# A written-out order of all engines, searched again with later transfers

## The chip, the cores and the metric

The kernel runs on one core of one Trainium2 chip. The metric is the device time of one execution in microseconds (us), lower is better. A row of the profile counts its times from the first instruction of the span.

## The reference

Two stages follow each other, for 8 batches of 576 positions. Stage 1 is attention in a window of 64 positions, 8 heads of 64; its output, 576 x 512 per batch, is the input x of stage 2. Stage 2 is a mixture of four attention experts: a gate picks two of the four for each position, and each expert projects x to q, k and v of 64 columns, attends causally over all 576 positions and projects back to 512 columns. All inputs and the output are float32.

```
rel = pos[:, None] - pos[None, :]
scores = np.where((rel >= 0) & (rel < 64), q @ k.T / 8, -1e9)          # stage 1, per batch and head
x = softmax(scores) @ v                                                # 576 x 512 per batch
for e in range(4):                                                     # stage 2
    q, k, v = x @ wq[e], x @ wk[e], x @ wv[e]
    ye = softmax(causal(q @ k.T / 8)) @ v @ wo[e]
    out += gate_weight[e] * ye                                         # zero where e is not in the top two
```

## The kernel before

Stage 1 goes by groups of four blocks of 64 queries, 72 groups in all; stage 2 by batch and by pair of experts (pr 0 and 1). Products of stage 2 are made with float16 pairs (a high and a low part), so that each is three matmuls (`three`, lines 582 to 584).

All work is cut into *units*, each a Python generator whose steps issue instructions for one engine or two. No scheduler reorders anything: the table `ORDER` (lines 41 to 142) names the units one after the other, and each time that a name stands there, the next step of that unit is issued. After a colon stand the PSUM banks that the step takes. Each engine does its own instructions in the order of the table, and waits by semaphores for what they need from other engines and from transfers.

```
for x in ORDER.split():
    x, _, y = x.partition(":")
    ...
    banks[:] = map(int, y)
    next(units[x], None)
```

The names that matter here, with the lines of their instructions:

- `p15` loads q and k of two heads as they lie in pair 15 of 16 (lines 181, 183). `m67` makes the scores of a group or two on PE (line 339). `q67` is the softmax of a group (DVE, POOL, ACT), `t` turns its result on PE (line 405) and masks it on DVE (line 408), `a` multiplies with v (PE line 430), then ACT and DVE write x as a float16 pair (lines 455, 457).
- `h15` loads the v windows of pair 15 (lines 190, 191) into one of three tiles `vt`. `n7` finds the largest magnitude in the two v tiles of batch 7, a step for each tile: one DVE reduction over 1,280 columns (line 473). Batch b takes the tiles of `h` 2b and 2b+1. The first step of `n7` reads `h14`'s tile, the second `h15`'s.
- `M`, `N` make scales of that, `v`, `k` and `r` are the projections of stage 2 (first PE, 12 matmuls of 260, 320 or 256 columns, lines 582 to 584; then ACT lines 602, 665 and DVE lines 608, 673). `g` is the gate.
- `x` makes scores of stage 2 (PE line 707), `y` their masked minimum and exponential (DVE line 718, ACT line 722), `u` scales the weights and splits them into a high and a low half (ACT line 769, POOL lines 779, 780).
- `D4021` (batch 4, pair 0, part 2, half 1) turns such a piece from tile `sp` to tile `tu` by a DMA transpose that SP issues (line 790). Part 0 is read by `A400`, parts 1 and 2 by `A401`: the product with v on PE (line 829). Its first two thirds read the high halves (last digit 0), its last third the low ones. `o` is the output projection, with a store at its end (lines 858, 862).
- `Fa`, `Fb` are matmuls whose result nobody reads (line 871); `f`, `c`, `i` write constants.

SP issues all transfers but three, in the order of the table, and waits before each until its tile is free; one that waits holds up those behind it. A transfer also waits for the eighth before it, since eight semaphores are used in turn.

Of the kernel before, what the change touches and what calls it, by code (L numbers as in the profile page):

```python
# [41 lines left out]
    'p0 f:01234567 i c p1 h0 h1 l0 l2 Fa0_4:0 m0:7 p1 z m2:6 q0 p0 q2 l1 l3 Fa1_4:5 m1:5 q0 q0 h2 e1 q0 m3:3 q1 q0 q1 '  # L42
    'q3 q2 q1 q1 q2 q3 n0 q3 q3 n0 q3 q1 q1 w0 q1 q2 n0 q1 Fa2_17:0 M0:5 w0:7 M0 q2 q1 t1:3 w0 d w2 M0 t1 q3 w0 e0 '
    'Fb3_2:4 w2:4 w2 Fb4_2:0 a1:34 M0 w2 w0 m4:56 a1 m6:72 q3 q4 w2 w1 a1 m8:1 q3 q4 p2 q5 q3 w1:3 q6 w3 t3:4 q5 q4 '
    'p3 w2 w1 q4 Fb5_1:0 w3:3 t3 w1 w3 q5 q5 Fb6_5:0 a3:34 s n1 q4 q5 v00:0 N0 w3 q5 q8 q5 q6 q5 a3 q7 m9:65 w1 q6 w3 '
    'q6 q6 q7 q5 v00 t5:7 q8 a3 q8 q7 q8 w3 q9 v01:3 q7 t5 q7 q8 m11:42 q9 v00 q7 v01 q8 q7 m13:17 q10 q9 q7 q9 q12 '
    'p4 q8 q7 q9 t7:0 q10 q11 v01 q10 q8 q10 q11 q10 Fb7_1:6 t8:3 q12 t7 q12 q12 a5:56 q10 q10 q12 q11 q10 t8 m15:20 '
    'a5 q10 q11 a5 t10:3 k000:4 q11 t10 q12 q13 k000 q13 k000 q12 q16 q13 r000:3 q12 q13 q14 a7:45 q14 r000 q14 r000 '
    'q14 a8:67 a7 q14 h3 r010:3 k000 q13 a7 h4 a8 q12 a8 q14 r000 t12:4 q14 r010 q15 v02:7 q15 q16 t12 q16 b0 v02 '
    'r001:6 q16 q15 n1 q14 q15 v03:4 q14 q16 n2 r001 k010:0 v03 q15 v02 r010 q16 g00 x004:2 k010 m19:73 n1 g00 r001 '  # L50
    'v03 k010 y004 y004 M1:5 g00 x000:41 k010 M1 q20 m17:02 q16 r010 y000 y000 y000 M1 g00 q16 k001:6 y000 q16 q18 '
    't14:1 q17 r001 q19 k001 q17 k011:4 k001 g00 q18 p5 g00 M1 q18 q17 q18 N1 t16:5 q19 q20 q18 r011:6 q20 k001 q17 '
    'g00 q20 q17 g00 q19 q20 k011 q18 r011 x014:0 x002:23 y014 k011 q18 q19 g00 y002 x001:04 k011 q19 a10:23 g00 y001 '
    'r011 a10 r011 m21:67 t14 p6 q20 y001 x011:40 a10 q18 q18 q21 y014 Fb8_2:1 a14:23 u000 q22 u000 y011 t17:1 a14 '
    'u000 u000 m23:40 y011 u000 q20 t17 q20 q21 t19:1 a14 u000 q21 q21 u000 q23 a12:23 q22 q21 q23 q23 q22 u000 v10:6 '
    'h5 a12 t16 u000 q22 u000 a12 a16:45 t19 u000 q22 u000 D0000 x003:23 y003 m25:71 u000 u000 a16 y003 a16 x010:23 '
    'k100:5 u000 D0001 y010 u000 q26 y010 y010 v11:4 u000 n2 v10 y010 r100:3 v10 q20 q25 k100 u010 n2 v11 u010 q22 '
    'k100 D0010 v12:2 u010 v11 u010 r100 u010 u010 r100 M2:6 u010 u010 x104:3 v12 A000:4 y104 M2 q23 v12 u010 q24 M2 '
    'A000 m27:32 A000 u010 q22 a17:45 M2 u010 u010 q23 y104 h6 a17 a17 q22 D0100 r110:6 q22 t21:4 q24 q25 r110 q25 '
    'v13:5 b1 r110 q25 q27 t21 u010 q25 v04:6 u010 n3 u010 u010 D0101 k101:4 v04 D0011 v13 g04 k110:7 q24 q28 g04 q24 '  # L60
    'v04 u010 v13 q24 v04 g10 k101 x012:06 g04 r101:5 y012 D0111 g10 k101 g04 q24 r111:6 g10 r101 D0110 g10 g04 g10 '
    'r101 g04 k110 q24 g10 g04 g10 k110 x013:40 g10 q24 g10 r111 A010:5 y013 p7 N2 y013 x100:74 g04 r111 g10 g04 '
    't23:0 q26 y100 k111:6 A010 q26 q24 y100 y100 u001 g04 q26 x101:71 A010 y100 u001 u011 q26 o00:5 u001 q27 q26 '
    'u011 q26 u001 q27 y101 q26 o01:4 q27 q26 k111 u011 o00 u001 k111 t26:1 o01 x114:7 t26 m29:56 u001 y114 q27 t25:7 '
    'q28 q29 D0020 q28 q30 x110:14 u001 q28 q29 q30 u011 q29 y110 Fb9_2:3 x102:53 q28 y102 y110 q30 D0021 q28 x103:25 '
    'u011 y110 u011 q30 y103 D0120 x111:34 q30 a19:12 q28 u011 y111 y103 a21:56 t23 y101 A001:3 u101 D0121 t25 q28 '
    'a21 q28 m31:04 a19 u100 a21 p8 t28:7 y111 a19 a23:56 o00 u100 q31 o01 u100 A001 A011:1 q32 h7 u100 A001 u100 '
    'A001 q31 u100 u101 a23 q32 u101 a25:23 q29 u100 u101 a23 A011 q32 u101 x113:56 a25 u100 A011 o03:4 A011 q29 a25 '
    't28 o02:1 q30 u100 u100 y110 x112:73 u100 u100 D1000 o02 y112 o03 v20:2 u101 y113 u100 k200:3 v20 D1020 y113 n3 '
    'u101 r200:6 D1001 k200 n3 q30 v22:5 q30 D1021 r200 r200 q30 v20 t30:6 u100 u100 k200 v22 M3:1 m35:32 u100 v22 '  # L70
    't30 y114 m33:45 D1010 q32 u110 q31 u110 A100:7 M3 q31 u110 q32 u100 p9 q31 M3 v21:6 D1011 A100 u110 M3 A100 u110 '
    'u110 x204:7 a26:01 y204 u110 u110 q36 y204 k210:7 a26 h8 u110 u110 v21 a26 o03 v23:0 u110 u110 v21 k210 k210 '
    'x200:61 u111 v23 u110 u110 u111 y200 y200 k201:7 v23 u110 q33 D1101 r211:0 y200 u110 q34 y200 D1100 k211:6 n4 '
    'k201 u111 u110 u111 g20 r211 r201:1 k211 r211 g20 D1111 q35 u111 r210:0 u111 k201 r201 g20 r201 k211 D1120 q33 '
    'x201:17 r210 y201 A110:6 g20 q32 g20 o02 u111 y201 A101:1 D1110 r210 q34 q32 q34 A110 m37:70 A110 A101 D1121 q32 '
    'q34 A101 A101 x214:6 g20 q34 q38 o10:1 q33 y214 q32 q37 q33 g20 N3 q33 t32:6 q35 q36 q35 o11:5 q36 o10 q34 q35 '
    'q34 q36 q34 o10 q35 A111:1 q36 g20 q34 o11 q36 q36 y214 g20 o11 q36 t34:3 q37 A111 q38 q37 A111 m39:25 g20 q36 '
    'q37 q38 A111 q38 a30:01 q39 p10 q37 t35:7 q39 u200 a30 o12:4 q39 t35 b2 q39 q40 o13:7 q38 o12 u200 a30 u200 q38 '
    'u200 q39 o12 q38 u200 o13 a28:01 q38 u200 o14:2 t32 a28 q38 u200 u200 a28 t37:4 x211:76 o14 t34 u200 u200 a32:01 '
    'h9 y211 u200 u200 a34:23 a32 D2000 a32 x210:67 u200 u200 a34 t37 v30:0 y211 u200 D2001 a34 m41:41 u200 y210 y210 '  # L80
    'D2010 y210 a35:23 v32:6 q40 q42 u200 y210 n4 v30 q40 D2011 r300:7 u210 a35 q40 a35 b3 q40 u210 o14 q41 r310:2 '
    'v30 v32 u210 q40 q41 h10 q40 q41 u210 q40 r300 v32 o13 t39:0 q40 r310 v31:5 u210 u210 t39 v33:4 u210 u210 q42 '
    'v31 r310 q42 u210 n4 u210 r300 q42 v31 x202:20 u210 u210 x212:65 y202 q42 x203:73 y212 v24:2 v33 u210 u210 y203 '
    'q41 k301:5 u210 u210 n5 y203 D2110 M4:1 x213:70 k311:3 D2100 v24 u210 M4 k301 y213 k310:6 q41 g24 D2101 q42 q42 '
    'g24 g30 r301:0 q42 v24 k310 D2111 y213 k301 k311 g30 g24 v33 M4 q42 m43:57 M4 g24 v24 N4 g24 g30 r301 k300:2 q43 '
    'p11 g30 g24 g30 q43 g30 k311 u201 g24 q43 r301 r311:3 u211 q43 u201 g30 g24 g24 g30 k310 k300 g24 u211 q43 q44 '
    'g30 m45:06 r311 k300 u201 g30 u201 r311 x314:4 x304:1 q45 x301:25 u211 u201 u201 y301 A200:3 u211 D2020 A210:2 '
    'A200 y304 y301 A200 t41:1 q44 u211 y314 q44 x300:35 q45 A210 q44 A210 o20:4 u211 q44 y300 q45 q44 q45 o21:7 q46 '
    'u201 q44 q45 o20 y300 y300 x302:03 a37:45 y302 q44 o20 D2021 o21 m47:20 t41 u211 a37 x303:73 D2120 y300 a37 '
    't43:1 y303 a41:45 y304 q44 o21 y314 u300 q47 A201:3 q46 a41 u300 y303 D2121 u300 a41 q46 q48 t44:7 u300 v40:4 '  # L90
    'q47 q48 A201 t44 q48 q46 u300 A201 m49:75 q47 q46 A201 q48 a39:23 q49 q46 u300 q46 q46 A211:6 a39 t43 h11 u301 '
    'q48 u300 p12 u301 a39 a43:01 A211 u301 q46 u301 A211 o23:2 A211 a43 u301 u300 q50 a43 v40 o22:6 q47 u301 u300 '
    't46:0 q49 q50 n5 D3020 o22 v41:1 o23 q49 x310:26 t46 u301 q49 q49 q47 u300 x311:30 y310 v41 v42:7 u300 q50 u300 '
    'y311 y310 D3000 k410:3 q48 u300 u300 v41 y310 y311 D3021 k400:2 q48 u300 D3001 q50 y310 q50 v40 x312:16 q48 u300 '
    'm51:54 y312 q50 u310 v42 u300 a44:01 k410 k400 k410 q51 r400:6 h12 a44 q50 u310 q52 q48 D3011 a44 t48:3 q51 u310 '
    'k400 q50 u310 k401:0 o22 n5 u310 u310 v42 r400 q52 D3010 t48 q52 u310 u310 v43:7 q52 q52 n6 u310 u310 r410:3 v43 '
    'q51 k401 r400 u310 u310 q51 k401 g40 M5:2 m53:06 D3100 v43 r410 u310 u310 x404:7 k411:4 r410 y404 q51 M5 o23 q53 '
    'q54 q50 D3101 M5 x313:57 u310 u310 y404 M5 x400:13 k411 y313 D3110 y313 y400 r411:2 u310 k411 t50:7 q53 y400 q54 '
# [888 lines left out]
```

## Time and profile before

| | us |
|---|---|
| runs of the kernel before | 421.39, 419.54, 418.27; median 419.54 |
| the profiled execution | 419.1 |
| its span, from the first to the last instruction | 417.4 |
| PE busy with matmuls | 387.8 |
| DVE, ACT, POOL busy | 343.5, 331.8, 303.3 |

The profiled execution took 1.7 us beyond its span. "Busy" counts the time in which at least one instruction of the engine runs; matmuls are pipelined, so the end of one is modelled. The views below tell, for an engine's idle time, which instruction or transfer ended it. A row of the timeline reads: start, length, engine, line, operation, tile written and tiles read, shapes, count, and in brackets the idle time of the engine before it with what ended that.

### The profile page before, as it was taken

The numbers are of one execution on the slowest core, as the hardware profiler recorded it, in microseconds if no ns is written. First come the engines' busy times: TensorE is split into PE (matmuls) and PEld (weight loads), VectorE is DVE, ScalarE is ACT, GpSimd is POOL, SyncE is SP. The second block draws the span as 40 slices with busy tenths as digits, with TensorE's granted clock in tenths as the row PEclk, the third lists the DMA queues.
The fourth block names the chain that finished last, engine by engine and source line by source line (L and its number), as shares of the span: only waits on it lengthen the run. The fifth ranks groups of instructions, "written<-read, shape, count | busy, mean of one in ns | idle before, by whom it ended". The sixth has DMA issues, their size and how long they took to land. (4 is left out here: it accounts for less than half of the span.)

```text
span 417.4 us, 17928 instructions
## 1 busy us (share of the span) xinstructions
PE 387.8 (93%) x7108; PEld 291.4 (70%) x7108; DVE 343.5 (82%) x1044; ACT 331.8 (80%) x1150; POOL 303.3 (73%) x682
## 2 busy tenths in 40 slices
PE   8978999998899989999999997989899999999875
PEld 6856876785486866777677775678667876776554
DVE  5999899969997586898988898679787799689962
ACT  1978668975997868987899799677798689969962
POOL 7477557886978977888968987678787985977320
PEclk9999999999999999999999999999999999999999
DMA  7963333868499986789589977599918874599993
GB/s 250 361 220 127 121 109 124 146 120 185 93 196 214 277 185 205 128 175 226 104 174 214 198 119 204 193 207 187 203 73 161 142 125 88 129 164 172 176 186 126
DMA packets 141731, 71.02 MB, mean 170 GB/s; under 512 B 122576, under 2 KB 125648, under 8 KB 141648
## 3 DMA queue, kind: packets, MB, share of 16 engines
q1 hardware_dynamic: 141280, 69.50, 77.0%
q8 instruction: 55, 0.90, 0.9%
q10 hardware_dynamic: 368, 0.39, 0.3%
q14 instruction: 28, 0.23, 0.2%
HBM read 30.94 MB, written 9.44 MB: 97 GB/s over the span
## 5 line engine op out<-in xcount | busy, mean ns | idle before, releaser
L780 POOL TENSOR_TENSOR sp<-p,sp 128x320 f16<-128x320 f32 (+3 forms) x110 | 100.7, 916 | 9.2
L722 ACT ACTIVATE p<-p,r 128x448 f32<-128x448 f32 (+3 forms) x128 | 77.6, 613 | 5.2 <-DVE r L718 4.8
L769 ACT ACTIVATE sp<-p,r 128x192 f16<-128x192 f32 (+3 forms) x122 | 73.6, 623 | 4.9 <-POOL r L758 2.1
L367 ACT ACTIVATE p<-ps,st 128x64 f32<-128x64 f32 x204 | 61.5, 320 | 17.6 <-POOL st L364 17.3
L779 POOL TENSOR_SCALAR p<-p,r 128x320 f32<-128x320 f32 (+3 forms) x110 | 65.3, 594 | 9.8 <-ACT sp L769 8.4
L718 DVE CUSTOM_DVE_ANT_0 p<-ps,causal,sc 128x320 f32<-128x320 f32 (+2 forms) x128 | 63.5, 544 | 6.3 <-PE ps L707 4.9
L408 DVE TENSOR_TENSOR pt<-ps,tri 128x1024 f32<-128x1024 f32 (+1 forms) x40 | 44.2, 1107 | 5.7 <-PE ps L405 5.1
L392 POOL TENSOR_TENSOR p<-p,st 128x256 f32<-128x256 f32 x72 | 43.6, 614 | 6.7 <-DVE st L388 5.1
L829 PE MATMUL ps<-tu,v 128*64 128x64 f16 (+2 forms) x1056 | 39.3, 229 | 4.6 <-DMA tu<-sp 3.8
L367 ACT ACTIVATION_READ_ACCUMULATOR p<-ps,st 128x1 f32 x204 | 43.5, 213 | 0.0
L707 PE MATMUL ps<-kt,qt 64*128 64x320 f16 (+3 forms) x480 | 40.6, 292 | 2.5 <-DVE v L608 1.2
L829 PEld LDWEIGHTS <-v 128*64 128x64 f16 x1056 | 35.8, 111 | 9.8 <-issue 5.7
L339 PE MATMUL ps<-k,q 64*32 64x96 f32 (+2 forms) x2304 | 37.5, 245 | 4.7 <-DMA k<-in_kT_dram 1.7
L582 PE MATMUL ps<-xh,wqhi 128*128 128x256 f16 (+1 forms) x128 | 36.6, 286 | 3.2 <-DVE qt L673 2.3
L430 PEld LDWEIGHTS ps<-pt,vt 64*64 64x64 f32 x1440 | 33.7, 133 | 7.5 <-issue 1.8
L430 PE MATMUL ps<-pt,vt 64*64 64x128 f32 (+1 forms) x1440 | 38.1, 249 | 0.7 <-DVE largest L271 0.4
L339 PEld LDWEIGHTS ps<-k,q 64*32 64x32 f32 x2304 | 29.9, 106 | 11.3 <-issue 5.2
L582 PE MATMUL ps<-xh,wkhi 128*128 128x320 f16 (+1 forms) x128 | 36.6, 286 | 0.0
L584 PE MATMUL ps<-xh,wklo 128*128 128x320 f16 (+1 forms) x128 | 36.6, 286 | 0.0
L583 PE MATMUL ps<-xl,wkhi 128*128 128x320 f16 (+1 forms) x128 | 36.6, 286 | 0.0
L584 PE MATMUL ps<-xh,wqlo 128*128 128x256 f16 (+1 forms) x128 | 36.6, 286 | 0.0
L583 PE MATMUL ps<-xl,wqhi 128*128 128x256 f16 (+1 forms) x128 | 36.6, 286 | 0.0
(167 smaller groups left out, 1027.2 us busy)
## 6 DMA issues: line engine op xcount, KB each, us to landing
vt<-in_vW_dram SPq DMA_DIRECT2D x16, 576.0 KB, 5.9
q<-in_qT_dram SPq DMA_DIRECT2D x14, 576.0 KB, 4.9
k<-in_kT_dram SPq DMA_DIRECT2D x14, 576.0 KB, 6.0
out_dram<-out SPq DMA_DIRECT2D x30, 256.0 KB, 3.5
tu<-sp SPq DMA_TRANSPOSE x93, 4.5
out_dram<-out SPq DMA_DIRECT2D x9, 128.0 KB, 2.6
q<-in_qT_dram SPq DMA_DIRECT2D x2, 320.0 KB, 7.0
k<-in_kT_dram SPq DMA_DIRECT2D x2, 320.0 KB, 6.5
```

The lines of the kernel that those rows point to most:

```text
L339: nc.tensor.matmul(S1[g][o:o + 32, i, c:c + n], lhsT=q_t[r, i % 2, q0:q0 + 32], rhs=k_t[r, i % 2, k0:k0 + n], start=True, stop=True)
L367: nc.scalar.activation(pt[:, i], ps[:, i, 64:128], AF.Exp, bias=st[:, 0, z + i:z + i + 1], scale=0.125, accum_out=st[:, 1, z + i:z + i + 1])
L430: nc.tensor.matmul(to, lhsT=values[d][r, h, b + e - (w == 0)], rhs=rhs, start=(e, h) not in started, stop=s == n - 1, skip_group_check=True)
L582: nc.tensor.matmul(ps, lhsT=ah, rhs=bh, start=first, stop=False)
L583: nc.tensor.matmul(ps, lhsT=ah, rhs=bl, start=False, stop=False)
L584: nc.tensor.matmul(ps, lhsT=al, rhs=bh, start=False, stop=last)
L718: nc.vector.tensor_tensor_reduce(out=dst, in0=src, in1=mask, scale=SC[b][:, 3:4], scalar=above, op0=OP.add, op1=OP.min, accum_out=to)
L722: nc.scalar.activation(p, p, AF.Exp, bias=r2[:, 0, x:x + 1], scale=-1.0, accum_out=r2[:, 1, x:x + 1])
L769: nc.scalar.activation(hi, p, AF.Copy, scale=by)
L779: nc.gpsimd.tensor_scalar(p, p, by, 1.0, op0=OP.mult, op1=OP.mult)
L780: nc.gpsimd.tensor_tensor(lo, p, hi, op=OP.subtract)
L829: nc.tensor.matmul(to, lhsT=V2[b % 2][:, c, a, 2 * pr + h], rhs=rhs, start=n == 0, stop=n == len(work_list) - 1, skip_group_check=True)
```

## The change

Only the table `ORDER` differs: the sequence of the steps on all engines and the PSUM bank numbers. Every unit, tile and instruction is the same, but for the matmuls that nobody reads: 40 calls before, 32 now. The change says of itself that the new sequence was searched with every transfer counted as landing later than on the mean.

The table is replaced as a whole. Here stand the lines that hold `h15` and the second `n7` (the load of a v tile and the reduction that reads it), of the table before and of the new one:

```diff
-    'a61 u510 q64 o43 h15 u510 u500 a61 m67:70 a59 D5000 q65 u510 x503:56 a59 q65 v62:1 u510 u510 y503 D5010 u510 '
-    'u510 y503 q66 v61:5 q67 D5001 q64 u510 n7 v62 r600:6 v61 u510 u501 q68 q66 q65 q64 q66 k600:3 u501 v62 u501 r600 '
...
+    'u500 a61:34 q65 a59 q65 m67:10 a59 u500 a61 q66 x503:56 u500 a61 D5001 k600:7 q65 u510 h15 y503 u500 y503 q65 '
+    'o42 u510 q66 D5010 x513:34 y513 r610:6 k600 u510 q64 u510 q66 k600 o43 y513 u510 q64 q68 q64 q67 v61:7 q64 u510 '
+    't64:4 q67 q68 r610 u510 v62:3 v61 u501 t64 v61 u510 q66 u510 u510 v60:5 v62 u510 r610 u510 n7 v60 r600:6 D5100 '
```

A name with a colon issues matmuls; between `h15` and this `n7` the table before has four of them (m67, x503, v62, v61), the new one six (x513, r610, v61, t64, v62, v60).

DVE around that reduction (tile `mv_7` from tile `vt0`), in the table before:

```order
L351 COPY_PREDICATED ps_67<-win_91,ps_67 128x2x64
L351 COPY_PREDICATED ps_67<-win_91 128x2x64
L473 TENSOR_REDUCE mv_7_5649<-vt0_84 128x1
L354 COPY_PREDICATED ps_67<-win_91,ps_67 128x4x64
L378 TENSOR_REDUCE st1_65_6378<-p1_65_6379 128x4
L756 RECIPROCAL r2_1_120<-r2_1_120 128x2
L608 SCALAR_TENSOR_TENSOR v2_0_116<-ps_67,v2_0_116 128x256 x2
L673 SCALAR_TENSOR_TENSOR qt0_105<-ps_67,qt0_105 128x320
L362 TENSOR_REDUCE st1_67_6551<-ps_67 128x4
```

DVE around the same reduction in the new table:

```order
L372 TENSOR_REDUCE st1_67_6519<-ps_67 128x4
L408 TENSOR_TENSOR pt1_64_6542<-ps_67,tri_92 128x1024
L608 SCALAR_TENSOR_TENSOR v2_0_116<-ps_67,v2_0_116 128x256
L673 SCALAR_TENSOR_TENSOR qt1_106<-ps_67,qt1_106 128x320
L473 TENSOR_REDUCE mv_7_5587<-vt0_84 128x1
L374 TENSOR_TENSOR p1_68_6522<-ps_67,st1_67_6519 128x256
L608 SCALAR_TENSOR_TENSOR v2_0_116<-ps_67,v2_0_116 128x256
L756 RECIPROCAL r2_1_120<-r2_1_120 128x2
```

One of the two evictions of v (line 608) and one of a projection of q (line 673) now stand ahead of the reduction; before, all of them stood behind it.

SP around the load of q and k of pair 13 (`q13`, `k13`), which stage 1 reads in `m57`, in the table before:

```order
L790 DMA_TRANSPOSE tu10_82<-sp10_77 128x11x128
L790 DMA_TRANSPOSE tu11_83<-sp12_79 128x8x128 x2
L790 DMA_TRANSPOSE tu11_83<-sp11_78 128x10x128 x2
L181 DMA q13_5158<-in_qT_dram 128x2x576
L183 DMA k13_5159<-in_kT_dram 128x2x576
L862 DMA out_0_dram<-out_3_0_5166 128x512
```

SP around the same load in the new table:

```order
L790 DMA_TRANSPOSE tu10_82<-sp10_77 128x11x128 x2
L790 DMA_TRANSPOSE tu11_83<-sp12_79 128x8x128
L181 DMA q13_4865<-in_qT_dram 128x2x576
L183 DMA k13_4866<-in_kT_dram 128x2x576
L790 DMA_TRANSPOSE tu11_83<-sp12_79 128x8x128
L790 DMA_TRANSPOSE tu11_83<-sp11_78 128x10x128 x2
```

The load has moved ahead of three transposes (one of tile `sp12`, both of `sp11`).

## Rows read from the trace of the kernel before

**Rows 1.** The page, part 1: busy time of each engine.
```profile
PE 387.8 (93%) x7108; PEld 291.4 (70%) x7108; DVE 343.5 (82%) x1044; ACT 331.8 (80%) x1150; POOL 303.3 (73%) x682
```
**Rows 2.** The waits: engine, line, waited for, us, times, longest.
```profile
DVE mv L473 <- DMA vt<-in_vW_dram: 9.7, 8, 2.0
...
PE ps L829 <- DMA tu<-sp: 3.8, 3, 1.5
```
**Rows 3.** The timeline of DVE: reductions of v that waited for their load.
```profile
52.63 1.49 DVE L473 TENSOR_REDUCE mv<-vt 128x1 f32<-128x1280 f32 x1 [1.12 <-DMA vt<-in_vW_dram]
...
93.10 1.49 DVE L473 TENSOR_REDUCE mv<-vt 128x1 f32<-128x1280 f32 x1 [1.69 <-DMA vt<-in_vW_dram]
...
147.12 1.49 DVE L473 TENSOR_REDUCE mv<-vt 128x1 f32<-128x1280 f32 x1 [1.78 <-DMA vt<-in_vW_dram]
...
233.74 1.49 DVE L473 TENSOR_REDUCE mv<-vt 128x1 f32<-128x1280 f32 x1 [0.57 <-DMA vt<-in_vW_dram]
...
272.86 1.49 DVE L473 TENSOR_REDUCE mv<-vt 128x1 f32<-128x1280 f32 x1 [1.11 <-DMA vt<-in_vW_dram]
...
319.76 1.49 DVE L473 TENSOR_REDUCE mv<-vt 128x1 f32<-128x1280 f32 x1 [1.98 <-DMA vt<-in_vW_dram]
```
**Rows 4.** The timeline of PE: idle times that a DVE instruction ended.
```profile
54.50 1.00 PE L339 MATMUL ps<-k,q 64*32 64x96 f32 x64 [0.56 <-DVE v L608]
...
96.24 0.56 PE L707 MATMUL ps<-kt,qt 64*128 64x320 f16 x5 [1.20 <-DVE v L608]
...
149.26 0.30 PE L582 MATMUL ps<-xh,wqhi 128*128 128x320 f16 x1 [1.32 <-DVE qt L673]
...
236.01 1.00 PE L339 MATMUL ps<-k,q 64*32 64x96 f32 x64 [0.48 <-DVE kt L673]
...
275.54 0.27 PE L582 MATMUL ps<-wvhi,xt 128*128 128x260 f16 x1 [1.13 <-DVE pt L408]
...
323.08 0.30 PE L582 MATMUL ps<-xh,wqhi 128*128 128x320 f16 x1 [1.02 <-DVE qt L673]
```
**Rows 5.** The timeline of PE: idle times that a transfer ended, and one beside.
```profile
30.18 0.96 PE L339 MATMUL ps<-k,q 64*32 64x32 f32 x64 [0.96 <-DMA k<-in_kT_dram]
...
258.25 0.43 PE L339 MATMUL ps<-k,q 64*32 64x32 f32 x24 [0.71 <-DMA k<-in_kT_dram]
260.46 0.39 PE L582 MATMUL ps<-wohi,y 128*128 128x512 f16 x1 [1.78 <-DVE pt L408]
...
299.85 0.41 PE L829 MATMUL ps<-tu,v 128*64 128x256 f16 x4 [1.49 <-DMA tu<-sp]
...
399.45 0.63 PE L829 MATMUL ps<-tu,v 128*64 128x256 f16 x12 [1.07 <-DMA tu<-sp]
...
404.46 0.45 PE L829 MATMUL ps<-tu,v 128*64 128x256 f16 x10 [1.20 <-DMA tu<-sp]
```
**Rows 6.** The page, part 6: transfers, count, KB each, median us from issue to landing.
```profile
vt<-in_vW_dram SPq DMA_DIRECT2D x16, 576.0 KB, 5.9
...
k<-in_kT_dram SPq DMA_DIRECT2D x14, 576.0 KB, 6.0
...
tu<-sp SPq DMA_TRANSPOSE x93, 4.5
```
**Rows 7.** The timeline of PE: two v projections, then one of q, then k.
```profile
315.53 0.28 PE L582 MATMUL ps<-wvhi,xh 128*128 128x260 f16 x1
...
318.20 0.30 PE L582 MATMUL ps<-xh,wqhi 128*128 128x320 f16 x1
...
319.83 0.30 PE L582 MATMUL ps<-xh,wkhi 128*128 128x320 f16 x1
```
**Rows 8.** The timeline of PE at the start: matmuls that nobody reads.
```profile
4.51 1.92 PE L871 MATMUL ps<-px 128*128 128x128 f32 x8
...
10.38 4.06 PE L871 MATMUL ps<-px 128*128 128x128 f32 x34
```
**Rows 9.** The page, part 2: granted clock in 40 slices.
```profile
PEclk9999999999999999999999999999999999999999
```

195 rows, old and new, of the table ORDER are left out of this document.

## Prediction

> **What bounds the kernel now.** I read the busy times first: PE is busy for 387.8 of the 417.4 us of the span, DVE for 343.5, ACT and POOL for less [rows 1]. So PE is the bound, and 29.6 us of its span is idle. Matmuls and their number stay, but for some that nobody reads, so a new order can only win idle time of PE: at the very most 29.6 us, and less, since at both ends of the span PE has no work yet or no more.
>
> Next I read who waits for transfers, since the change counts these as later. The list of waits has two such groups of weight. DVE waits 9.7 us in 8 places, at the reduction `n` (line 473), for the load of the v tile; PE waits 3.8 us in 3 places for a transposed piece `tu` [rows 2]. The reader is to see that the larger group is not PE's: it costs nothing until PE runs out of work.
>
> Then the timeline, to see whether PE does. Six reductions wait, at 52.63, 93.10, 147.12, 233.74, 272.86 and 319.76, for 0.57 to 1.98 us, 8.25 us together [rows 3]. Two to four us behind each, PE stands and is released by a DVE instruction that the order puts behind that reduction: 0.56, 1.20, 1.32, 0.48, 1.13 and 1.02 us, 5.71 us together [rows 4]. PE stands some 70% as long as DVE did; the rest was hidden by work that PE still had. Last come PE's own waits for transfers: 0.96 and 0.71 us for k, and 1.49, 1.07 and 1.20 us for `tu`, 5.43 us together [rows 5]. So 11.1 us of the 29.6 us goes back to transfers. The wait of 1.78 us at 260.46 [rows 5], two us behind the late k, is put down to DVE; I do not count it to the 11.1.
>
> **The loads of v.** Both orders have 16 loads and 16 reductions; what changes is how much PE work the order puts between them. I count that work by the spacing of such steps in the trace: from one step of v to the second after it 2.67 us, so 1.3 us for a v step, and 1.6 us for a q step [rows 7]; other steps likewise. For `h15` and the second step of `n7`, the table before has m67 0.6, x503 0.4, two v steps 2.6: 3.6 us. The new table has x513 0.4, r610 1.6, two steps of `t` 0.4 together with two v steps and one more 3.9, thus 6.5 us by unrounded spacings. A load takes 5.9 us from issue to landing in the median [rows 6]; 3.6 is too little, and the reduction waited 1.98 us. (3.6 + 1.98 = 5.6, so the two views agree.)
>
> By the same count, the six reductions of [rows 3] go, in order of time: from 4.4 to 6.8 us, from 4.7 to 4.7, from 6.0 to 12.2, from 3.1 to 6.5, from 4.0 to 8.7 and from 3.6 to 6.5. Five of them pass 5.9 us; the second, `h6` to the first half of batch 3, does not move. I therefore take away five of the six idle times of [rows 4], 0.56 + 1.32 + 0.48 + 1.13 + 1.02 = 4.5 us, and leave the 1.20 at 96.24. Two of the five pass by only 0.6 us, and a load that is issued late because SP is held up is not seen in such a count. The bounds for this term are 2 us (only the two large leads, and half the rest) and 5.7 us (all six).
>
> The Trainium skill has a rule against this term. Its page "DMA: Bandwidth & Descriptors", section "Anatomy of one DMA — SWDGE (gpsimd) path", gives one transfer about 2.0 us of fixed cost plus its bytes at 436 GB/s, for 576 KB an estimate of 2.0 + 1.35 = 3.4 us. By it nearly every lead of before would have been long enough, the waits would have other causes, and the new order would gain nothing here. The trace disagrees: such loads took 5.9 and 6.0 us [rows 6], and these six readers did wait; the measurement decides.
>
> **PE's own waits for transfers.** k at 30.18: the lead falls from 5.0 to 4.4 us, so its 0.96 us stays and may grow by 0.6. k at 258.25 is pair 13, which SP now issues three transposes earlier, and its readers stand later: the lead goes from 4.9 to 16.2 us, and 0.7 us goes. `tu` at 299.85 is `D4021`, whose lead goes from 2.8 to 4.1 us, and the low half is read last; of the 1.49 us I take 1.2 away. A transpose lands 4.5 us after its issue in the median [rows 6], so 4.1 is near enough to leave something. The two at the tail: for 399.45 the pieces of batch 7, pair 0 lose as much lead as they win (one from 3.5 to 3.0, one from 5.0 to 3.0, one from 3.5 to 6.0), for 404.46 one goes from 1.6 to 2.5, the other from 4.0 to 2.5. I take nothing for these 2.3 us, with bounds of 1 us won and 2 us lost. Over all 96 pieces the mean lead is the same (11.6 and 11.7 us), but 9 instead of 18 lie under 4 us, so no new wait of this kind is likely.
>
> **What the new order puts in their place.** Every step moved brings its other waits along. Counted in the two orders, PE has 212 places where it can wait for DVE before and 207 now; in 94 before and 107 now it has no work of its own between the step that gives DVE its input and the one that takes the result. The trace does not have the new places, so the price of one lies between nothing and what PE loses here when DVE is late, 0.5 to 1.3 us [rows 4]. Even with DVE held for 8.25 us [rows 3], 30% stayed hidden, and DVE is idle for 18% of the span [rows 1], so most of the 13 more should cost nothing. I take two of them, at the lowest of the six prices: 2 × 0.5 = +1.0 us, a choice rather than a reading. Bounds: −1 us (the 5 places fewer may take waits of their own away) and +3 us (the two at the highest price).
>
> **Dummy matmuls, start and end.** Forty calls that nobody reads become 32. They are only worth something if they are not hidden; all but the first lie in front of work for which PE would otherwise wait, so taking them out turns busy time to idle time, and the sum takes 0. At the start 8 calls (before: 8 in two groups, then 17) [rows 8] stand ahead of the first scores; POOL writes one constant before the tile that they read. With them at 0.24 us each as at first, or twice that, and the constant ahead or beside, I work out for the first scores between 1.1 us earlier and 1.4 us later: 0, with these as bounds. At the end both orders have the same chain of output, 0.
>
> **The sum.** Of the profiled execution's 419.1 us: − 4.5 (v loads) − 0.7 (k) − 1.2 (`tu`) + 1.0 (new places) + 0 (start, tail) = **413.7 us**. The profiled execution lies 0.4 us below the median of the three runs, 419.5, so nothing is to be put right. About 1% (4.2 us) can be told from no change here; 413.7 is 1.4% below, just outside.
>
> **The rivals.** *More goes.* The 1.78 us at 260.46, the 1.20 at 96.24 and the tail go too: all of 11.1 + 1.8 us, with the places at nothing: 406 us, and up to 410. For it speaks that a search looked at all transfers; against it, that three leads stay under the landing time.
>
> *No change.* The waits were not what set the time: DVE's reduction comes on time, and PE then waits for the next thing in the same stretch, DVE's own queue. For it: DVE is busy 82% of the span, and PE's gaps are shorter than the waits before them, so a part is already slack. If the DVE term gives 2 us instead of 4.5, with the bounds +1.5 more elsewhere, it is 419.1 − 2 − 1.9 + 2.5 = 417.7. The skill's rule above ends here too, at 419.
>
> *Slower: PE on the heels of DVE.* The order is laid for late transfers, and PE steps now follow closer on DVE steps. If all 13 more places cost 0.85 us, the middle of 0.48 to 1.32 [rows 4], it is 419.1 − 6.4 + 11 = 423.7 us. It decides where more than seven such places show a wait (7 × 0.85 = 6). Against it: the largest of PE's gaps behind DVE, those of [rows 4] and the 1.78 of [rows 5], all stand shortly behind a late transfer.
>
> *Slower: a cold start.* PE's granted clock shows 9 in all slices [rows 9], with the many dummy matmuls at the start; the first eight took 0.24 us each, the later ones 0.12 [rows 8], so PE began at half pace, 1.2 of 2.4 GHz, and was at full pace by 10.4. With 17 calls fewer ahead of the first scores it could go longer at half pace. If the first 30 us did so, some 12 us of matmuls would cost twice as long, and some 6 us of that would fall into idle time: about 425 us.
>
> **How the numbers follow.** Forecast, 0.52, own range 410.5 to 416.5: most of it (0.40) is faster by over 1% (below 415.3), the rest (0.12) within. More goes: 0.09, faster. No change: 0.24, within 1%. DVE's heels: 0.11, of which 0.10 is slower by over 1% (above 423.7) and 0.01 within. Cold start: 0.04, slower. Thus faster 0.49, same 0.37, slower 0.14. For the range I go from 408.5, which leaves out the better part of the first rival, to 421.5, which leaves out the two slower ones and holds no change.
>
> **What would show it.** Right: DVE's waits for v loads fall from 9.7 us to 3 or less, one is left near 95 us, and PE's idle times behind them are gone; the scores of pair 13 do not wait for k; PE's waits for `tu` lie at the tail only; PE's idle time is about 24 us. Wrong: DVE's waits go but PE's idle time stays near 30 us, with other releasers (no change); PE's waits for DVE (lines 408, 608, 673, 718) grow, and no DVE wait for a transfer stands ahead of them (heels); matmuls of the same shape before 35 us last twice as long (cold start). A load that is issued later than its place, because SP stands before a transpose, would show as a wait of the reduction in spite of a long lead.

## The result and the profile after

The changed kernel takes 415.82 us in the median of 14 runs (412.69 to 417.47), the kernel before 420.47 us in as many: a ratio of 0.9884, 95% interval 0.9849 to 0.9918. That is 1.2% faster, 4.65 us between the medians, where 5.4 us were forecast. The profiled execution took 415.31 us, with a span of 413.6 us, 3.8 us less than before.

Page, part 1, and a row of its part 3, of the changed kernel:

```profile
PE 386.8 (94%) x7092; PEld 288.8 (70%) x7092; DVE 340.3 (82%) x1044; ACT 332.6 (80%) x1150; POOL 301.8 (73%) x682
...
q8 instruction: 55, 0.90, 0.9%
```

PE is busy 1.0 us less than in [rows 1] and idle for 413.6 − 386.8 = 26.8 us instead of 29.6. The sum went down by only 2.8 us, but what it consists of has changed. Part of it is hidden by the matmuls that nobody reads: they alone kept PE busy for 10.1 us before and 7.2 us after (counted from the traces). Without them, the time in which PE does no useful work fell by 5.7 us, from 39.7 to 34.0, and the useful matmuls took 1.9 us longer, 379.6 instead of 377.7; together that is the 3.8 us of the span. The waits of the changed kernel (engine, line, waited for: us, times, longest):

```profile
PE ps L339 <- issue: 5.9, 3, 2.6
PE ps L214 <- DVE half L207: 3.0, 1, 3.0
PE ps L829 <- DMA tu<-sp: 2.1, 4, 1.4
PE ps L405 <- ACT p L367: 1.9, 2, 1.1
PE ps L405 <- POOL p L392: 1.9, 4, 0.6
DVE mv L473 <- DMA vt<-in_vW_dram: 1.3, 2, 1.0
PE ps L797 <- ACT sp L769: 1.1, 2, 0.9
```

The waits of DVE for v fell from 9.7 us [rows 2] to 1.3. Summed by the engine waited for, PE's waits for DVE fell from 14.3 to 6.3 us (3.0 of these, and 1.1 of those before, are the very first instruction, which has nothing ahead of it to hold up), those for transfers from 5.5 to 2.1. Against that stand waits for ACT, from 1.1 to 4.1 us, for POOL, from 1.1 to 1.9, and the first row: idle time that the profile ends with nothing, from 1.6 to 5.9 us. The wait for `tu` at A401 is still there, as in [rows 5]:

```profile
295.91 0.52 PE L829 MATMUL ps<-tu,v 128*64 128x256 f16 x6 [1.44 <-DMA tu<-sp]
```

The largest wait of PE without a cause stands in the middle of one step, m55, after 39 of its recorded matmuls. Timeline of PE in the changed kernel (start, length, instruction, count, idle time before):

```profile
240.80 1.29 PE L829 MATMUL ps<-tu,v 128*64 128x256 f16 x32
242.01 0.27 PE L480 MATMUL ps<-ident,mv 128*1 128x128 f32 x1
242.21 0.58 PE L707 MATMUL ps<-kt,qt 64*128 64x320 f16 x6
242.73 0.75 PE L339 MATMUL ps<-k,q 64*32 64x96 f32 x39
246.10 0.54 PE L339 MATMUL ps<-k,q 64*32 64x96 f32 x25 [2.63 <-issue]
246.57 0.44 PE L582 MATMUL ps<-wohi,y 128*128 128x512 f16 x1
246.80 0.63 PE L583 MATMUL ps<-wolo,y 128*128 128x512 f16 x1
247.23 0.63 PE L584 MATMUL ps<-wohi,y 128*128 128x512 f16 x1
```

Behind it the matmuls of 512 columns follow each other at 0.43 us, and the busy time by stretch (PE, PEld, DVE, ACT, POOL, granted clock, share of DMA, GB/s) says why:

```profile
240.00:246.80 6.80, 4.17 (x138) 3.21 (x135) 4.64 (x18) 5.57 (x24) 5.67 (x10) 1.00 1.22 173
246.80:250.20 3.40, 3.40 (x12) 1.39 (x12) 1.71 (x7) 0.79 (x2) 0.24 (x1) 0.50 0.49 110
```

For 3.4 us the granted clock is 0.50, the lower level of 1.2 GHz. A second such stretch begins at 397.0, behind waits of 0.94 and 0.46 us at line 797, where PE itself turns the last pieces by matmuls. Until its last matmul, the profile before has no such stretch; so some of the 1.9 us that the useful matmuls took longer lies here.

### The profile page after: what moved, and what is told of

Read it like the earlier page. It is cut to its first block, busy times and chain, and to the rows that moved or that the text cites. A ratio compares the mean times of both kernels' runs of the same rounds, so it can differ in the third digit from the quotient of the medians.

```text
span 413.6 us, 17936 instructions
## 1 busy us (share of the span) xinstructions
PE 386.8 (94%) x7092; PEld 288.8 (70%) x7092; DVE 340.3 (82%) x1044; ACT 332.6 (80%) x1150; POOL 301.8 (73%) x682
## 5 line engine op out<-in xcount | busy, mean ns | idle before, releaser
L722 ACT ACTIVATE p<-p,r 128x192 f32<-128x192 f32 (+3 forms) x128 | 77.4, 609 | 9.9 <-DVE r L718 9.6
L769 ACT ACTIVATE sp<-p,r 128x448 f16<-128x448 f32 (+3 forms) x122 | 73.4, 620 | 3.8 <-POOL r L758 2.6
L392 POOL TENSOR_TENSOR p<-p,st 128x256 f32<-128x256 f32 x72 | 43.6, 617 | 13.4 <-DVE st L388 10.8
L829 PE MATMUL ps<-tu,v 128*64 128x64 f16 (+2 forms) x1056 | 39.7, 231 | 2.1 <-DMA tu<-sp 2.1
L582 PE MATMUL ps<-xh,wkhi 128*128 128x256 f16 (+1 forms) x128 | 36.7, 287 | 0.0
L584 PE MATMUL ps<-xh,wklo 128*128 128x256 f16 (+1 forms) x128 | 36.6, 286 | 0.0
L583 PE MATMUL ps<-xl,wkhi 128*128 128x256 f16 (+1 forms) x128 | 36.6, 286 | 0.0
```

Of the source, the lines that this page charges most:

```text
L582: nc.tensor.matmul(ps, lhsT=ah, rhs=bh, start=first, stop=False)
L583: nc.tensor.matmul(ps, lhsT=ah, rhs=bl, start=False, stop=False)
L584: nc.tensor.matmul(ps, lhsT=al, rhs=bh, start=False, stop=last)
L722: nc.scalar.activation(p, p, AF.Exp, bias=r2[:, 0, x:x + 1], scale=-1.0, accum_out=r2[:, 1, x:x + 1])
L769: nc.scalar.activation(hi, p, AF.Copy, scale=by)
L829: nc.tensor.matmul(to, lhsT=V2[b % 2][:, c, a, 2 * pr + h], rhs=rhs, start=n == 0, stop=n == len(work_list) - 1, skip_group_check=True)
```

## The experiments

The theory to be tested was that of the forecast: late loads of v hold DVE, PE stands behind it, and the new order wins by giving these loads time. Its rivals were that PE would have waited for DVE in any case, or that the gain lies elsewhere. In the pieces of the table below, "-" is the old place and "+" the new one. Each run gives a ratio to the kernel before on the same chip.

**after_again, after_3: the changed kernel twice more.** No edit.

> The changed kernel once more, as the measure for the runs beside it. Both theories: about 416 us, 1.2% under the kernel before. If PE's stall of 2.63 us in the middle of m55 (at 246.10 in the first profile) comes from where the program's text lies, it stands there again, at about 2.6 us, and so does the one of 1.55 us in m23 at 69.92; if these were accidents of one execution, they are gone or elsewhere.

> The changed kernel a third time, as the measure for the runs beside it: about 415 us. All theories: the stalls in m55 (1.9 to 2.6 us so far) and m23 (1.3 to 1.6 us) stand there again, and 3.4 us at half clock behind the one in m55.

Measured: 0.9895 (0.984 to 0.995) and 0.9864 (0.9818 to 0.9909). The stall in m55 was 1.87 and 1.93 us, always with 25 recorded matmuls behind it, each time with half clock right after; the one in m23 1.26 and 1.23 us. So these belong to the program, not to one execution. A401 waited again for D4021, 1.41 and 1.43 us, and in after_again also 1.56 us for D4020 just ahead of it. One wait for v had stayed in the changed kernel and grew: that of the reduction which stood at 233.74 before [rows 3]. It was 1.03 us in the first profile, 1.70 and 1.86 in these two, and here PE stood behind it again, for 0.87 and 1.04 us. Timelines of DVE and PE in after_3:

```profile
226.47 1.49 DVE L473 TENSOR_REDUCE mv<-vt 128x1 f32<-128x1280 f32 x1 [1.86 <-DMA vt<-in_vW_dram]
```

```profile
228.41 0.30 PE L582 MATMUL ps<-xh,wqhi 128*128 128x320 f16 x1 [1.04 <-DVE qt L673]
```

**b_late_n: the reductions later.** One of the six places (the others alike):

```diff
- q67 D5001 q64 u510 n7 v62 r600:6 v61
...
- u501 u510 r610:6 t64 k600
...
+ u501 u510 r610:6 n7 t64 k600
```

> The table before with one thing changed: the six reductions of v that waited for their loads come later, so that 8 to 10 us of PE work lie between load and reduction (before 3 to 6). Theory (the waits of these reductions make PE's six idle times): DVE's waits for v fall from 9.7 to under 3 us, the six idle times of 5.7 us go, and the time falls by 4.5 to 5.7 us, 1.1 to 1.4%. Rival (PE would have waited for DVE in the same places anyway): the waits go, the time stays within 1.5 us of before, and PE's idle time stays near 30 us with other releasers.

Measured: 1.0022 (0.9986 to 1.0058), no gain at all, although DVE's waits for v fell to 1.1 us. The rival had it right for this run. The timeline of DVE in this kernel shows where the reduction of 96 us went, and the timeline of PE what came of it:

```profile
96.06 1.47 DVE L473 TENSOR_REDUCE mv<-vt 128x1 f32<-128x1280 f32 x1
...
98.31 0.55 DVE L718 CUSTOM_DVE_ANT_0 p<-ps,causal,sc 128x320 f32<-128x320 f32 x1
```

```profile
98.92 0.27 PE L582 MATMUL ps<-xh,wqhi 128*128 128x256 f16 x1 [1.85 <-DVE m L718]
```

The 1.20 us at 96.24 [rows 4] are gone, but 1.5 us of reduction now stand ahead of the two operations of line 718 for which PE waits next, and that wait grew from 0.62 to 1.85 us. This is one place of six; the others were not followed up. Behind the first 45 us, in which the two tables are the same, PE was idle for 17.1 us until its last matmul instead of 18.8. The run took away the wait and moved 1.5 us of DVE's work at once; it doesn't tell the two apart. The next one does.

**b_no_wait: the same order, other data.**

```diff
-values[2 * b + x]
+values[2 * b + x - ((b, x) in ((2, 0), (3, 0), (4, 0), (6, 0), (6, 1), (7, 1)))]
```

> The table before, with the six reductions of v that waited for their loads reading the tile of the pair before, which lies there long since; the order of all engines is untouched. (Left out by this: six scales come from other data.) Theory (the waits make PE's idle times behind them): DVE's waits for v fall to some 1.5 us, PE's six idle times of 5.7 us go, 1.1 to 1.4% less time. Rival (what the late n run showed: PE waits for the next thing instead, since DVE has its own work to catch up): the waits go, but PE's idle time falls by under 2 us, and the time by under 0.5%.

Measured: 0.9929 (0.9888 to 0.997), 3.0 us less (1.3 to 4.7). Page, part 1, and the waits:

```profile
PE 386.6 (94%) x7107; PEld 291.1 (71%) x7108; DVE 344.0 (84%) x1044; ACT 331.8 (81%) x1150; POOL 303.0 (74%) x682
```

```profile
PE ps L829 <- DMA tu<-sp: 3.1, 3, 1.5
...
PE ps L582 <- DVE pt L408: 1.8, 1, 1.8
DVE mv L473 <- DMA vt<-in_vW_dram: 1.4, 2, 1.0
```

The span was 410.3 us, so PE was idle for 23.7 us: 5.9 less than before, and all six idle times of [rows 4], 5.7 us, are gone from its timeline. The waits of DVE do make PE's. In time it came to about two thirds of the 4.5 us that were forecast for five of the six, with an interval that holds them, and to half of the 5.7 us of idle time, which the interval leaves out. The profile is of one of the shortest executions, 413.12 us, at a granted clock of 0.999. The 1.8 us of line 408 that are left are those at o33.

**a_early_n and a_late_h: the waits put back into the new table.** First with the reductions forward (one of five places), then with the loads back:

```diff
-r610 u510 n7 v60 r600:6 D5100
...
-q67 v61:7 q64 u510 t64:4
...
+q67 v61:7 n7 q64 u510 t64:4
```

> The new table with five of these reductions moved forward until the lead over their loads is that of the table before (3.4 to 6.3 us of PE work). Theory: the waits come back to some 7 us in five places, PE stands behind them for 4 to 5 us, and the time rises by 4 to 5 us over the new table, to about the time before. Rival (the gain of the new table has another source): within 1.5 us of the new table.

```diff
-D5001 k600:7 q65 u510 h15 y503 u500
...
-q67 v61:7 q64 u510 t64:4
...
+q67 v61:7 h15 q64 u510 t64:4
```

> The new table with five loads of v moved back (h4, h8, h12, h13, h15) until the lead is 2.7 to 5.9 us of PE work; the order of PE, DVE, ACT and POOL is untouched. Theory: waits of some 7 us come back, PE loses 4 to 5 us, so 1.0 to 1.2% over the new table. Second theory (from the run with early reductions, which lost 17 us): in the new order DVE and PE stand so close that a late reduction costs PE more than its wait, and the clock with it: 7 to 15 us, 1.7 to 3.5%. Rival (loads don't matter): within 1.5 us of the new table.

Measured: a_early_n 1.0314 (1.0259 to 1.0369), 17.8 us over the new table run beside it, which neither theory had. a_late_h 0.9932 (0.989 to 0.9973), about 0.5% over the new table's 0.9884, in the direction of the theory, but with half of its size, and the intervals overlap: that later loads alone cost time in the new order is not shown. The waits of the two, a_early_n first:

```profile
DVE mv L473 <- DMA vt<-in_vW_dram: 10.8, 4, 3.3
PE ps L582 <- DVE xl L457: 7.2, 2, 3.9
...
PE ps L707 <- DVE kt L673: 3.1, 3, 2.7
PE ps L582 <- DVE qt L673: 2.3, 1, 2.3
```

```profile
DVE mv L473 <- DMA vt<-in_vW_dram: 7.2, 3, 3.4
...
PE ps L582 <- DVE p L374: 2.6, 1, 2.6
PE ps L430 <- DVE v L608: 1.7, 1, 1.7
```

In a_early_n the reductions stand in another place of DVE's work as well. Its 10.8 us of waits and the moved work cost PE 13.3 us in five gaps, one of them (1.06 us) behind a reduction that did not wait. Five stretches of 3.4 us at half clock lie in the span ahead of the last matmuls, three of them at these gaps and one behind the stall in m55, and the clock granted over it is 0.977. How much of the 17.8 us is wait, place and clock was not taken apart. The profile of a_late_h is of its longest execution, 420.61 us, at a granted clock of 0.981; it shows the waits, and not the time of the median run. In a_late_h, where DVE's order is that of the new table, three of five loads came late. One of the three waits, 1.55 us, is no longer than the changed kernel has there without this edit (1.03 to 1.86 us); behind the other two PE lost 4.3 us. Two loads with a lead of 4.3 and 5.9 us came in time, one with 4.6 us, behind the load of pair 14 and a transpose on SP, made a wait of 3.4 us: PE work between load and reader alone doesn't tell the landing.

**b_p13 and b_p13_3: q and k of pair 13 earlier.** Past seven transposes, and past three:

```diff
- o31:5 q56 g40 A301 p13 q52 q53 y414 A301 o30 t52:1
...
+ M5:2 m53:06 p13 D3100 v43 r410
```

> The table before with the load of q and k of pair 13 moved ahead, behind m53, past seven transposes on SP. Theory: PE's wait of 0.71 us at m57 goes, and the 1.78 us at o33 two us behind it stays, 0.2% less. Rival: the 1.78 us was a consequence of the late k (m57, then its softmax and t52 on DVE stood back): both go, 2.5 us or 0.6% less. A third way: the transposes behind it on SP come later, and A301 or A311 waits for them by as much.

```diff
- o31:5 q56 g40 A301 p13 q52 q53 y414 A301 o30 t52:1
...
+ q54 r401:4 y400 p13 D3111 r411
```

> The table before with the load of pair 13 moved ahead of three transposes only, as in the new table, behind the piece that A310 waits for. Theory (the 1.78 us at o33 followed from the late k, and the loss of b_p13 was the 3.3 us wait of A310 for its transposed piece): the waits at m57 and o33 go, none comes at A310, and the time falls by 2 to 2.5 us, 0.5 to 0.6%. Rival: another transposed piece comes late by as much, and the time stays within 0.2% of before.

Measured: b_p13 1.0053 (1.0017 to 1.0089), b_p13_3 0.9863 (0.9803 to 0.9923). Both waits went together in both runs, that for k and the 1.78 us at o33. In b_p13 another took their place (timeline of PE), and the timeline of SP has its cause:

```profile
249.89 0.78 PE L829 MATMUL ps<-tu,v 128*64 128x256 f16 x17 [3.31 <-DMA tu<-sp]
```

```profile
239.90 1.65 SPq L790 DMA_TRANSPOSE tu<-sp  x1
241.60 1.08 SPq L862 DMA_DIRECT2D out_dram<-out  x1
242.78 9.56 SPq L790 DMA_TRANSPOSE tu<-sp  x5
```

The piece that A310 waits for was issued at 242.78 and landed at 249.85, 7.1 us later, where the median is 4.5 [rows 6]. In the kernel before it stood first in this row of the timeline of SP and landed at 242.09:

```profile
237.60 13.45 SPq L790 DMA_TRANSPOSE tu<-sp  x5
```

So it landed 7.8 us later: 5.2 us because SP issued it later (1.0 us of that is how late SP already was 15 us earlier, ahead of the moved load), and 2.6 us because it took longer. The third way that the expectation named is what happened, at A310 instead of A301 or A311. Three transposes later (b_p13_3) there is no such wait; m57 runs through:

```profile
256.31 0.94 PE L339 MATMUL ps<-k,q 64*32 64x96 f32 x64
```

The time fell by some 1.4%, more than the 0.6% expected. The trace accounts for 2.1 us of it (PE's idle time is 413.3 − 385.8 = 27.5 us instead of 29.6), and for 2.0 us less of busy time; with six runs the interval reaches from 0.8 to 2.0%, and what lies beyond 2.5 us stays unexplained. This one moved load thus measures what the whole new table measures beside it, 0.9864, and the two can't be told apart. Sums of idle time are coarse, too: in the first 45 us, which all runs of the old order share, PE was idle for 6.6 us in the profile before and for up to 8.4 in the others.

**b_all: all three at once.** b_no_wait and b_p13, and A401 behind the first step of o40:

```diff
- y510 u411 A401:0 q63 A410 A400 A410 A400 y510 o40:6 M6
...
+ y510 u411 q63 A410 A400 A410 A400 y510 o40:6 A401:0 M6
```

> All three removed together in the table before: the six waits of the reductions (other data, as above), k of pair 13 loaded ahead, and A401 behind the first step of o40. Theory (my sum without its price for new places): 6.4 us less, 1.5%, thus as fast as the new table or faster. Rival: what the new order gained lies in how PE and DVE follow each other and not in the transfers; then under 2.5 us, 0.6%.

Measured: 0.9881 (0.9843 to 0.9918), the ratio of the new table. The wait for D4021 went; o40 then waited 0.9 us for the result of A400. A310 lost 3.1 us to its late transpose, as in b_p13:

```profile
PE ps L829 <- DMA tu<-sp: 4.5, 3, 3.1
...
PE ps L582 <- ACT y L835: 0.9, 1, 0.9
```

So the edits of the forecast's three terms, in the order of before, are together worth what the whole new order is worth, as far as intervals some 0.7% wide can tell. That doesn't say that the new order wins by nothing else, nor how the gain divides among the three: b_no_wait gave 0.7%, b_p13_3 1.4%, b_p13 a loss.

**a_m55, a_m55_2, a_best: the stall without a cause, and a try at more.**

```diff
- g40 x402:36 m55:10 y402 A301 y410 q52 D3121 q54 o30:3 q52
+ g40 x402:36 y402 A301 y410 q52 D3121 q54 o30:3 m55:10 q52
```

> The new table with m55 moved behind the first step of o30, whose six matmuls of 512 columns last 2.6 us. Theory (PE ran out of instructions, since the 64 short matmuls of m55 follow other short ones and the next piece of the program's text had been fetched less than 1 us before): the stall in m55 falls from 2.6 us to under 1 us and the half clock behind it (246.8 to 250.2) goes, so 2 to 4 us less than the new table. Rival (the stall is tied to m55 itself, or comes and goes by chance): it stands in m55 at its new place, and the time is that of the new table within 1.5 us.

> The new table with m55 behind the first step of o30, a second time, for a narrower interval. Its first profile had no stall in m55 and no half clock behind it, but 1.05 us more at o30 and 0.94 us more at x401, both waiting for DVE. Theory: the two give back about half, so it is 1 to 2.5 us under the new table run beside it. Rival: all of it is given back, within 0.5 us.

Measured: 0.9894 (0.9836 to 0.9953) and 0.9893 (0.985 to 0.9936), beside 0.9895 and 0.9864 for the changed kernel in the same two groups of runs. Neither profile has a stall in m55, nor half clock behind it; a_m55's waits:

```profile
PE ps L339 <- issue: 2.9, 2, 1.5
...
PE ps L582 <- DVE m L718: 1.1, 1, 1.1
...
PE ps L707 <- DVE y L838: 0.9, 1, 0.9
```

The stall went as expected, and the time did not: two waits for DVE give back 2.0 us, and no difference can be told from none. The rival of a_m55_2 stands. a_best has A401 behind the first step of o40 in addition:

```diff
- x504:6 A401:3 q62 q63 g50 D4121 y510 y504 q62 y501 q63 M6:6 g50 o40:0 q62
+ x504:6 q62 q63 g50 D4121 y510 y504 q62 y501 q63 M6:6 g50 o40:0 A401:3 q62
```

> The new table with m55 behind the first step of o30, and A401 behind the first step of o40, so that its transposed piece has 2.6 us more to land. Theory: PE's wait of 1.4 us for D4021 goes, and o40 waits up to 0.9 us for the result of A400 instead (as it did in the run with all three removed): 0.5 to 1.4 us under a_m55_2 and 1.5 to 4 us under the new table, which would make it faster than both kernels. Rival: given back at once, within 0.5 us of a_m55_2.

Measured: 0.9849 (0.9801 to 0.9897), beside 0.9864 for the new table. The wait for D4021 is gone, and a new one of 1.42 us for DVE stands shortly ahead of where it was (timeline of PE in a_best):

```profile
293.62 0.27 PE L480 MATMUL ps<-ident,mv 128*1 128x128 f32 x1 [1.42 <-DVE r L718]
```

It is faster than the kernel before, but not shown to be faster than the new table.

## Why the prediction came out as it did

**The forecast of 413.7 us, from an execution of 419.1, was 1.3% less; 1.2% less was measured.** The sign and the size held, and the likeliest case came about. Not all of its terms did.

*Loads of v, −4.5 us.* The mechanism is shown: with the waits taken away and the order untouched (b_no_wait), PE's six idle times go and the time falls by 3.0 us (1.3 to 4.7). In the first profile of the new table they are gone too, all six: the one that I left standing, 1.20 us at 96 us, went as well. Its lead did stay 4.7 us by my count, and the load landed 5.3 us after its issue in both, but DVE came to the reduction 5.2 us after that issue instead of 3.7, and waited for 0.29 us. At 233.74 it went the other way: the lead by my count rose from 3.1 to 6.5 us, yet DVE came 4.0 to 4.2 us after the issue in the three profiles, the load landed after 5.1 to 5.8 us, DVE waited longer than before, and in two of them PE stood behind it, 0.87 and 1.04 us. I had also left out, without saying so, a wait of 1.25 us at 129.74 that PE hardly felt: the one idle time of note in the three us behind it, at 132.75, is 0.24 us. The lead in PE work was good enough for a forecast of the sum, and not for single loads.

*k of pair 13, −0.7 us.* Mis-sized. I saw the 1.78 us at o33 two us behind the late k and did not count it, since the profile gave it to DVE. Both b_p13 kernels lose the two together: the late scores had pushed softmax and t52 back. The term should have been −2.5 us. The other wait for k, 0.96 us at 30.18, which I left in, is gone in the profile after and 0.45 us in after_again.

*`tu` at 299.85, −1.2 us.* This step failed. The lead rose from 2.8 to 4.1 us as read, but the piece landed 6.9 us after its issue, not the 4.5 us of the median, and PE waited for 1.4 us in all three profiles of the new table. I had taken the median for a transfer that stands in a row of five behind a load of q and k. It stood behind that load in the old order as well, and the trace of before already has 6.2 us for it (issued at 293.58, landed at 299.80).

*The tail, 0.* Held: the two waits of 2.3 us for `tu` are gone, and waits at line 797 rose from 0.7 to 1.9 us.

*Start and end, 0.* At the start this held: DVE took up the first scores at 8.7 us, 0.1 us later than before. At the end it did not: from PE's last matmul to the end of the span it is 4.24 us before and 5.09 us in the changed kernel. ACT's last eviction was released by PE before, and by one of DVE's now (timelines of ACT, before and after):

```profile
413.30 0.47 ACT L858 ACTIVATE out<-ps,sc 128x256 f32<-128x256 f32 x1 [0.64 <-PE ps L584]
```

```profile
409.52 0.47 ACT L858 ACTIVATE out<-ps,sc 128x256 f32<-128x256 f32 x1 [1.11 <-DVE out L856]
```

*New places, +1.0 us.* The sign held, the place did not. PE's waits for DVE did not rise; those for ACT and POOL did, by 3.8 us together. I had counted places that wait for DVE alone. About half of the 6.0 us that PE now waits for these two lie in the first 40 us, where the matmuls that nobody reads became fewer; how much of it these had only hidden was not taken apart.

*What had no term at all.* Idle time without a cause rose by 4.3 us, in m23 and m55, with half clock behind the second. Together with the last two items and with `tu` this took back what the v loads and k had won beyond the forecast: −5.7 − 2.5 of waits stood in the first profile, against −4.5 − 0.7 in the sum. That these errors nearly cancel is luck.

*The rivals.* "No change" is refuted by b_no_wait, yet b_late_n shows its mechanism at work: where the reduction's own 1.5 us lie decides as much as its wait. "On DVE's heels" did not come: PE's waits for DVE fell. a_early_n shows that it could have, at 17.8 us for five reductions in the wrong place. The cold start did not come, as the first scores show.

*The page's rule.* By 3.4 us for a load of 576 KB, an estimate from the Trainium skill's "DMA: Bandwidth & Descriptors", next to nothing could have been won at these six places; the runs show the contrary, and the loads of v took 5.2 us in the median in the profile after. That section is about transfers which GpSimd issues; these are issued by SP. The same page's section "Queues, rings and completion order" says that SP's transfers share one row of rings, whose entries each DMA engine takes in their order. b_p13 fits that: the transpose issued 4.4 us behind the load of k took 7.1 us from issue to landing, where without that load ahead it had taken 4.5; the rings themselves do not show in the traces.

## What to carry to other kernels

Where the bound engine waits for an engine that waits for a transfer, the transfer can be the cause, also when a step or two lie between: read on upstream until nobody waits, and test the chain by taking away the wait alone, as b_no_wait does. Its price is less than the waits: 9.7 us on DVE were 5.7 us of idle time on PE and 3.0 us (1.3 to 4.7) of time. Before a reader is moved away from a late transfer, look at what stands behind its new place; b_late_n took away 8.6 us of waits and won nothing. And count a transfer's landing from its own place in the queue, with what is issued just ahead of it, rather than by a median.

## What was not expected of the hardware

PE can stand in the middle of a step in which nothing is waited for. It did so in m6 and m23, and in m55 in all five profiles that have it at its place in the new table, for 0.9 to 2.6 us, each time among matmuls of which 64 take 1.00 us together. The queue "q8 instruction" moved 55 packets of 16 KB (0.90 MB), one for every 260 or so of PE's matmuls and weight loads, and a packet began 0.9 us before the stall in m55, at 242.54. In the three profiles of the changed kernel each of the nine such stalls began 0.4 to 1.1 us after a packet of this queue; behind most packets there is none. With six matmuls of 512 columns ahead of m55 it did not stand. That PE had run out of instructions fits all of this; that it is the cause was not shown by itself, and whether it costs time stays open, since a_m55 gave it back to DVE.

Some gaps of PE were followed within 1 us by 3.4 us at half clock, with 0.43 us from one matmul of 512 columns to the next, where a_m55 has 0.21 to 0.22 us at full clock. The length of the gap does not tell which: the gaps of 1.87 and 1.93 us in m55 were, one of 2.75 us in a_early_n and one of 2.45 us in a_best were not. Runs of one kernel differ in this as well: one of the changed kernel took 412.9 us with a granted clock of 0.999 over its span, and one 417.5 us with 0.984.
